# Two tiles through the first products together: x loaded ahead of the weights, k, v and q as double products

## The chip, the core and the metric

The kernel runs on one core of a Trainium2 chip. The metric is the device time of one execution in microseconds; a time of a kernel is the median of its runs. All times inside an execution are microseconds from the start of the profiled span. The core's engines are TensorE (PE, with its weight loads as PEld), VectorE (DVE), ScalarE (ACT), GpSimd (POOL) and SyncE (SP), which issues all the DMA of this kernel.

## The reference

Two layers, run twice with the same weights: a linear attention block and a PEER expert block, each with a layernorm in front and a residual behind. Tokens 2048, width 576, 32 heads of 18.

```python
x = A_x
x = x + _A_ref(_layernorm(x, axis=-1), A_wqkv, A_wo)
x = x + _B_ref(_layernorm(x, axis=-1), B_w_q, B_k1, B_k2, B_u, B_v)
x = x + _A_ref(_layernorm(x, axis=-1), A_wqkv, A_wo)
x = x + _B_ref(_layernorm(x, axis=-1), B_w_q, B_k1, B_k2, B_u, B_v)
```

In `_A_ref`, q, k and v are the three 576-column thirds of `layernorm(x) @ wqkv`. With phi(t) = (t + 1 for t > 0, else exp(t)) + 1e-6, each head sums phi(k)^T v over all tokens (the state), multiplies it by phi(q) and divides by phi(q) times the sum of phi(k); the result goes through wo. Only the very first products of the first layer, for tokens 0 to 383, are touched by the change.

## The kernel before

**Tiles.** The 2048 tokens are 16 tiles of 128. A tile of x is one load of 288 KB; it is normalized, transposed by TensorE in five blocks of 128 columns (576 columns, with 64 of the third block doubled), and multiplied by the weights.

**Two parts of every number.** Each transposed tile and each weight block is split into a high part, rounded by ScalarE (`split`, L110, or L115 for the third block), and a low part, the difference, by VectorE (L111, or L116; one block of k by GpSimd). A product (`product`, L220) adds up 14 passes of two matmuls each: five of high by high, four of high by low weight, five of low tile by high weight. With `by_block` the passes are sorted by weight block, so that a product can start when block 0 of the weights is there; before, only k of tile 0 uses it. In the profile `thif` and `tlof` are the parts of a tile, `whi` and `wlo` those of the weights, `ptf` the transposition, `ppk`, `ppv`, `ppq` the products.

**Weights.** `load_weight` (L134 to L137) loads five blocks for each of k, v and q, in six transfers, since the third block is loaded in two halves. They go to ten staging buffers: k and v fill them, and q's blocks reuse those of k, after k's splits. Later the `fold` loads reuse v's.

**Order.** On TensorE, ScalarE, VectorE and GpSimd the instructions run in the order in which the program writes them (`in_order`). SP's order is set by a planner at build time, from its own estimate of what is ready when. In the profile SP issues x of tile 0, the identity, k's blocks (six transfers), x of tile 1, v's blocks (six), x of tile 2, q's blocks (six), `kraw` (a small table of expert keys), two further small tables, x of tile 3, and then the first `fold` loads; counted in this order, x of tile 1 is the ninth transfer, `kraw` the twenty-third.

**The start.** 14 warm-up matmuls run on TensorE while the first load is under way. Then the program writes: statistics of tile 0 (`statistics`, L166 to L174: three small operations on VectorE, two on GpSimd, one on VectorE), normalization (`normalized`, L195, on ScalarE), transposition, two warm-up matmuls, k of tile 0 (block by block), tile 1's transposition, k of tile 1, v of tile 0 and 1, the state of tile 0 (`front_state`, L291), tile 2's transposition, q of tile 0, the state of tile 1, q of tile 1. Between them stand the weights' splits. k and q go through `phi` (L226 to L228: exp on ScalarE, two operations on VectorE); v is copied from PSUM by ScalarE in three pieces (L251, L253). `small_loads` gives GpSimd a row of preparations: two memsets, then L609, then L611, which waits for `kraw`, and three memsets and two copies behind it (the last is L621). Tile 2's statistics come behind these on GpSimd.

PSUM is four buffers of two banks each, shared by transpositions, products, warm-ups and the state sums; the state keeps one for as long as the first layer's loop lasts. From tile 2 on a loop takes one tile after the other (k, v, q, transposition of the next, state), together with the loads and products of the `fold`.

Of the kernel before, what the change touches and what calls it, by code (L numbers as in the profile page):

```python
# [27 lines left out]
CUT = 2 * HC  # L28
# [11 lines left out]
def blocks(rem):  # L40

    rows, at = [], 0
    for b in range(NB):
        rows.append((at, b - (b > rem)))
        at += 64 if b == rem else P
    return rows


def passes(rem):
    rest = [b for b in range(NB) if b != rem]  # L50
    return ([("hi", b, "hi") for b in range(NB)] + [("hi", b, "lo") for b in rest]
            + [("lo", b, "hi") for b in range(NB)])
# [6 lines left out]
def network(ctx, tc, x_in, wqkv, wo, wq_t, k_t, u_t, v2, c_mask, c_mask4, c_ident, c_code, c_code1, c_scale, c_shift, out):  # L59
# [7 lines left out]
    def psum(name):  # L67
        return ps.tile([P, 1024], F32, tag="ps", name=name)
# [5 lines left out]
        return t[:, 512 - CUT:512 - CUT + D]  # L74

    PARTS = (0, CUT, 512 - CUT), (CUT, D, 512)


    ident = cp.tile([P, P], F32, name="ident")
# [47 lines left out]
    def load_weight(src, c0, rem, name):  # L127

        tiles = []
        for b, (r, bl) in enumerate(blocks(rem)):  # L130
            st = stage(f"{name}st{c0}_{b}")
            cols = slice(c0, c0 + D)
            if b != rem:
                nc.sync.dma_start(st, src[r:r + P, cols])  # L134
            else:
                nc.sync.dma_start(st[:64], src[r:r + 64, cols])
                nc.sync.dma_start(st[64:], src[r:r + 64, cols])  # L137
            tiles.append(st)
        return tiles

    def split_weight(tiles, c0, hi, lo, rem, which=range(NB), eng=nc.vector):
        for b in which:
            cols = slice(c0, c0 + D)
            if b != rem:
                split(tiles[b], hi[:, b, cols], lo[:, blocks(rem)[b][1], cols], eng)
            else:
                split_mixed(tiles[b], hi[:, b, cols])
# [13 lines left out]
                                  reason="in_order")  # L161


    def statistics(xt, n, soon=False):
        st = wk.tile([P, 2, 6], F32, tag="st", name=f"st{n}")
        nc.vector.bn_stats(st[:, 0], xt[:, :HALF])  # L166
        nc.vector.bn_stats(st[:, 1], xt[:, HALF:])
        mv = wk.tile([P, 2], F32, tag="mv", name=f"mv{n}")
        nc.vector.bn_aggr(mv, st.rearrange("p a b -> p (a b)"))  # L169
        rs = wk.tile([P, 2], F32, tag="rs", name=f"rs{n}")  # L170
        nc.gpsimd.tensor_scalar(rs[:, 0:1], mv[:, 1:2], EPS_LN, 1.0, op0=ALU.add, op1=ALU.mult)  # L171
        nc.gpsimd.tensor_tensor(rs[:, 0:1], rs[:, 0:1], mhalf, op=ALU.pow)
        eng = nc.vector if soon else nc.gpsimd
        eng.tensor_scalar(rs[:, 1:2], mv[:, 0:1], rs[:, 0:1], -1.0, op0=ALU.mult, op1=ALU.mult)  # L174
        return rs

    def spread(xt, total, n):

# [9 lines left out]
        nc.gpsimd.tensor_tensor(rs[:, 1:2], m[:, 0:1], rs[:, 0:1], op=ALU.mult)  # L188
        return normalized(xt, rs, n)

    def normalized(xt, rs, n):

        y = wk.tile([P, 2, 320], F32, tag="y", name=f"y{n}", bufs=3)
        x2 = bass.AP(tensor=xt.tensor, offset=xt.offset, ap=[xt.ap[0], [256, 2], [1, 320]])
        nc.scalar.activation(y, x2, AF.Identity, scale=rs[:, 0:1], bias=rs[:, 1:2])  # L195
        return y.rearrange("p a b -> p (a b)")

    def transposed(y, n, more=None, tag="t", step=P):
# [11 lines left out]
        split(pt[:, :w], hi.rearrange("p a b -> p (a b)")[:, :w], lo.rearrange("p a b -> p (a b)")[:, :w])  # L210
        return hi, lo

    def product(tt, hi, lo, cols, n, parts=PARTS, rem=REM, by_block=False):

        o = psum(f"pp{n}")
        todo = sorted(passes(rem), key=lambda p: p[1]) if by_block else passes(rem)
        for i, (a, b, w) in enumerate(todo):
            wb = hi[:, b] if w == "hi" else lo[:, blocks(rem)[b][1]]
            for c0, c1, at in parts:
                nc.tensor.matmul(o[:, at:at + c1 - c0], tt[a == "lo"][:, b, :], wb[:, cols + c0:cols + c1],  # L220
                                 start=(i == 0), stop=(i == len(todo) - 1))
        return o

    def phi(p, n):
# [8 lines left out]
    ys = {}  # L233
    kva = {}
    wob = {}


    def front_T(l, t):
        tt["f", l, t] = yield from transposed(ys.pop(("f", l, t)), f"f{l}_{t}")

    def front_k(l, t):
        k = product(tt["f", l, t], whi, wlo, D, f"k{l}_{t}", by_block=(l == 0 and t == 0))
        yield
        tt["fk", l, t] = phi(k, f"k{l}_{t}")

    def front_v(l, t):
        v = product(tt["f", l, t], whi, wlo, 2 * D, f"v{l}_{t}", parts=((0, CUT, 0), (CUT, D, 512)))
        yield
        vt = v5[t % 2]
        for c, x in ((0, v[:, :2 * HC]), (4, v[:, 512:512 + 2 * HC])):  # L250
            nc.scalar.activation(vt[:, c:c + 4, :63], x.rearrange("p (c e) -> p c e", c=4), AF.Copy)  # L251
        yield
        nc.scalar.activation(vt[:, 8:, :36], v[:, 512 + 2 * HC:512 + 2 * HC + 72].rearrange("p (c e) -> p c e", c=2), AF.Copy)  # L253

    def front_q(l, t):
        q = product(tt["f", l, t], whi, wlo, 0, f"q{l}_{t}")
        yield
        fq = phi(q, f"q{l}_{t}")
        nc.sync.dma_start(pq_d[l][t], fq)
# [331 lines left out]
    def warm_up(n):  # L591

        p = psum("warm")
        for i in range(n):
            nc.tensor.matmul(p[:, :512], junk[:, :P], junk[:, :512], start=True, stop=True)

    def first_load(l, t):
        xt = wk.tile([P, D], F32, tag="x", name=f"xf_{t}", bufs=3)
        nc.sync.dma_start(xt, x_in[t * P:(t + 1) * P, :])
        xs["f", t] = xt  # L600

    def first_ln(l, t):
        xt = xs.pop(("f", t))
        ys["f", 0, t] = normalized(xt, statistics(xt, f"f0_{t}"), f"f0_{t}")

    def small_loads():
        for t in v5:
# [47 lines left out]
    def run(l, *seq):  # L655


        for f, t, *n in seq:
            if f is bc or ok(t):
                g = begun.pop((f, l, t), None) or (exp_T(l, *t) if f is bc else f(l, t))  # L660
                for i in range(n[0] if n else 99):
                    if g is None or next(g, bc) is bc:
                        break
                else:
                    begun[f, l, t] = g
# [31 lines left out]
    first_load(0, 0)  # L697
    nc.vector.memset(junk, 0.0)
    nc.sync.dma_start(ident, c_ident)
    wk_in = load_weight(wqkv, D, REM, "w")  # L700
    first_load(0, 1)
    wv_in = load_weight(wqkv, 2 * D, REM, "w")
    ET = mybir.EngineType
    ALL = ET.PE, ET.Activation, ET.DVE, ET.Pool
    with in_order(*ALL):
        x0, x1 = xs.pop(("f", 0)), xs.pop(("f", 1))
        warm_up(14)
        rs0 = statistics(x0, "f0_0", soon=True)
        split_weight(wk_in, D, whi, wlo, REM, (0,))
        ys["f", 0, 0] = normalized(x0, rs0, "f0_0")  # L710
        split_weight(wk_in, D, whi, wlo, REM, (1, 2))
        run(0, (fT, 0, 1))
        warm_up(2)
        run(0, (fT, 0))
        split_weight(wk_in, D, whi, wlo, REM, (3,), nc.gpsimd)
        rs1 = statistics(x1, "f0_1", soon=True)
        split_weight(wk_in, D, whi, wlo, REM, (4,))
        ys["f", 0, 1] = normalized(x1, rs1, "f0_1")
        run(0, (k, 0, 1), (fT, 1))
        split_weight(wv_in, 2 * D, whi, wlo, REM, (0, 1))  # L720
        run(0, (k, 0), (k, 1, 1))
        split_weight(wv_in, 2 * D, whi, wlo, REM, (2, 3, 4))
        first_load(0, 2)
        wq_in = load_weight(wqkv, 0, REM, "w")
        small_loads()
        first_load(0, 3)
        run(0, (k, 1), (v, 0, 1))
        split_weight(wq_in, 0, whi, wlo, REM, (0, 1))
        run(0, (v, 0))
        first_ln(0, 2)  # L730
        split_weight(wq_in, 0, whi, wlo, REM, (2, 3))
        run(0, (v, 1, 1))
        split_weight(wq_in, 0, whi, wlo, REM, (4,))
        run(0, (st, 0), (fT, 2), (v, 1), (q, 0), (st, 1), (q, 1))
        PER, FIRST = 8, 13
        for t in range(2, FIRST):
            m0 = PER * (t - 2)
            groups = [m for m in range(m0, m0 + PER) if m < 2 * H]
            done = (m0 - 1) // 16 if m0 % 16 == 0 and 0 < m0 <= 2 * H else None
            for m in groups:  # L740
                fold_load(m)
            if t + 2 < NT:
                first_load(0, t + 2)
            if t + 1 < NT:
                first_ln(0, t + 1)
            run(0, (k, t, 1))
            if done is not None:
                fold_out(done)
            run(0, (k, t))
            run(0, (v, t, 1))  # L750
            if done is not None and groups:
                fold_T(done)
            run(0, (v, t))
            if groups:
                run(0, (q, t), (fT, t + 1), (st, t))
            elif t < L:
                run(0, (fT, t + 1), (q if t < L - 1 else st, t), (st if t < L - 1 else q, t if t < L - 1 else -1))
            if done is not None and not groups:
                fold_T(done)
            for m in groups:  # L760
                fold_mm(m)
# [101 lines left out]
```

## Time and profile before

| what | value |
|---|---|
| runs | 745.76, 747.09, 747.62 us; median 747.09 |
| the profiled execution | 748.71 us, span 746.9 us |
| mean granted TensorE clock | 0.995 |
| busy: PE, PEld, DVE, ACT, POOL | 726.5, 675.2, 458.9, 289.7, 200.4 us |

The profile comes from one execution of its own. Busy times overlap between engines and don't add up to the span. A row of a timeline gives the start, the duration, the engine, the line, the operation, what is written and read, and in brackets the idle time of the engine before it and what ended that. A row with x2 or more is several instructions merged, with the duration from the first start to the last end. The chain of waits is read from the last instruction back, and shown in order of time: the work that set the end.

### The profile page before, as it was taken

How to read it: one execution, taken by the hardware profiler on the slowest of the kernel's cores; microseconds unless marked ns; L12 is line 12 of the kernel's file. 1: busy time of each engine (PE TensorE's matmuls, PEld its weight loads, DVE VectorE, ACT ScalarE, POOL GpSimd, SP SyncE). 2: the span in 40 equal slices, each digit the busy share in tenths (PEclk: the TensorE clock that was granted, in tenths of full speed). 3: DMA queues.
4: the chain of work that ended last, by engine and by line, in shares of the span. 5: the costliest groups of instructions: out<-in, count | busy, mean ns of one | idle time of the engine just before them, and what ended most of it. 6: DMA issues, size and time to landing. Idle time of an engine off the chain costs nothing.

```text
span 746.9 us, 14647 instructions
## 1 busy us (share of the span) xinstructions
PE 726.5 (97%) x5672; PEld 675.2 (90%) x5672; DVE 458.9 (61%) x1006; ACT 289.7 (39%) x588; POOL 200.4 (27%) x541
## 2 busy tenths in 40 slices
PE   7999999999999999999999999999999999999995
PEld 4999999999998889999999999999899999999884
DVE  3732332324236887666666666563366899999986
ACT  4523232332324544444444444452233333444343
POOL 2110001000003543333333333130033334533431
PEclk9999999999999999999999999999999999999998
DMA  9727546641121321222333212222634323121101
GB/s 256 251 81 247 197 159 216 232 130 50 49 64 32 111 99 68 99 86 83 89 104 105 87 68 84 84 72 68 176 87 119 104 83 116 32 88 41 48 33 65
DMA packets 52470, 79.64 MB, mean 107 GB/s; under 512 B 5616, under 2 KB 22512, under 8 KB 52400
## 3 DMA queue, kind: packets, MB, share of 16 engines
q1 hardware_dynamic: 52400, 78.70, 33.1%
q8 instruction: 45, 0.74, 0.4%
q14 instruction: 25, 0.20, 0.1%
HBM read 55.12 MB, written 23.56 MB: 105 GB/s over the span
## 4 chain that ended last, share of the span: by engine, by line
PE 82%; DVE 10%; ACT 3%; issue 2%; POOL 1%; DMA 1%; SPq 0%; DVEq 0%; POOLq 0%; ACTq 0%
PE ppk L220 15%; PE ppv L220 15%; PE ppq L220 13%; PE ppo L414 13%; PE pps L444 12%; PE kva L291 3%; PE fold_ps L560 2%; PE ptb L205 2%; PE ptf L205 2%; PE pto L205 2%; PE po L528 2%; DMA wst<-in_wqkv 1%; PE m L345 1%; DVE o L392 1%; DVE tlob L111 1%
## 5 line engine op out<-in xcount | busy, mean ns | idle before, releaser
L227 DVE TENSOR_SCALAR ek<-ek 128x576 f32<-128x576 f32 x32 | 15.1, 472 | 82.5 <-ACT ek L226 82.5
L220 PE MATMUL ppk<-whi,thif 128*128 128x252 f32 x320 | 50.3, 302 | 2.4 <-ACT thif L110 2.3
L220 PEld LDWEIGHTS ppk<-whi,thif 128*128 128x128 f32 x320 | 44.6, 191 | 6.8 <-ACT thif L110 3.4
L414 PE MATMUL ppo<-ohi,thio 126*128 126x252 f32 (+1 forms) x320 | 50.2, 299 | 0.1
L171 POOL TENSOR_SCALAR rsf<-mvf 128x1 f32<-128x1 f32 x16 | 3.1, 192 | 171.2 <-DVE mvf L169 171.0
L220 PE MATMUL ppk<-whi,tlof 128*128 128x252 f32 x320 | 48.2, 295 | 0.3 <-DVE tlof L111 0.3
L227 DVE TENSOR_SCALAR eq<-eq 128x576 f32<-128x576 f32 x32 | 15.6, 488 | 52.5 <-ACT eq L226 52.5
L220 PE MATMUL ppv<-whi,thif 128*128 128x252 f32 x320 | 47.4, 294 | 0.1
L220 PE MATMUL ppv<-whi,tlof 128*128 128x252 f32 x320 | 46.9, 293 | 0.0
L195 ACT ACTIVATE yb<-x,rsb 128x640 f32<-128x640 f32 x32 | 29.5, 923 | 44.3 <-POOL rsb L188 44.2
L444 PE MATMUL pps<-shi,thib 128*128 128x512 f32 x160 | 43.9, 404 | 2.0 <-ACT thib L110 2.0
L414 PEld LDWEIGHTS ppo<-ohi,thio 126*128 126x128 f32 (+1 forms) x320 | 44.8, 189 | 1.1 <-DVE eq L228 0.3
L220 PEld LDWEIGHTS ppk<-whi,tlof 128*128 128x128 f32 x320 | 44.9, 190 | 0.5 <-DVE tlof L111 0.5
L220 PEld LDWEIGHTS ppv<-whi,thif 128*128 128x128 f32 x320 | 43.9, 188 | 0.4 <-ACT thif L110 0.3
L220 PEld LDWEIGHTS ppv<-whi,tlof 128*128 128x128 f32 x320 | 43.9, 188 | 0.0
L181 ACT ACTIVATE junk<-x,mb 128x576 bf16<-128x576 f32 x32 | 24.7, 771 | 49.5 <-POOL mb L180 46.1
L444 PE MATMUL pps<-shi,tlob 128*128 128x512 f32 x160 | 42.7, 397 | 0.0
L449 ACT ACTIVATE s<-pps 128x512 f32<-128x512 f32 x32 | 19.1, 596 | 54.9 <-PE pps L444 54.9
L251 ACT ACTIVATE v<-ppv 128x252 f32<-128x252 f32 x64 | 20.9, 379 | 50.0 <-PE ppv L220 50.0
L220 PE MATMUL ppq<-whi 128*128 128x252 f32 (+1 forms) x260 | 39.6, 299 | 0.6 <-DVE eq L228 0.6
L404 DVE SCALAR_TENSOR_TENSOR x<-po,x 128x576 f32<-128x576 f32 x29 | 21.9, 753 | 29.3 <-PE po L528 28.3
L414 PE MATMUL ppo<-olo,thio 126*128 126x252 f32 (+1 forms) x256 | 39.5, 293 | 0.0
(155 smaller groups left out, 1788.9 us busy)
## 6 DMA issues: line engine op xcount, KB each, us to landing
fold<-in_wq_t SPq DMA_DIRECT2D x64, 288.0 KB, 4.8
whi<-hl_d SPq DMA_DIRECT2D x26, 320.0 KB, 3.4
pq_d<-eq SPq DMA_DIRECT2D x19, 288.0 KB, 2.2
pq<-pq_d SPq DMA_DIRECT2D x19, 288.0 KB, 3.1
xf<-in_x SPq DMA_DIRECT2D x16, 288.0 KB, 5.4
x<-in_x SPq DMA_DIRECT2D x16, 288.0 KB, 2.7
x_d<-x SPq DMA_DIRECT2D x16, 288.0 KB, 3.3
x<-x_d SPq DMA_DIRECT2D x16, 288.0 KB, 2.7
```

The costliest lines, as they stand in the source:

```text
L181: nc.scalar.activation(junk, xt, AF.Square, bias=m[:, 0:1], accum_out=m[:, 1:2])
L195: nc.scalar.activation(y, x2, AF.Identity, scale=rs[:, 0:1], bias=rs[:, 1:2])
L205: nc.tensor.transpose(pt[:, b * P:(b + 1) * P], x, ident)
L220: nc.tensor.matmul(o[:, at:at + c1 - c0], tt[a == "lo"][:, b, :], wb[:, cols + c0:cols + c1], start=(i == 0), stop=(i == len(todo) - 1))
L227: nc.vector.tensor_scalar(e, e, 1.0, EPS, op0=ALU.min, op1=ALU.add)
L251: nc.scalar.activation(vt[:, c:c + 4, :63], x.rearrange("p (c e) -> p c e", c=4), AF.Copy)
L291: nc.tensor.matmul(a[64 * h:64 * h + 64, c * 72:c * 72 + n], vt[:, 2 * c + h], fk[:, f0:f0 + n], start=(t == 0 and c == 0), stop=(t == NT ...
L404: nc.vector.scalar_tensor_tensor(y, row(p), 0.0, xt, op0=ALU.add, op1=ALU.add, accum_out=total)
L414: nc.tensor.matmul(p[:, at:at + c1 - c0], hl[a][:r, b], w[:r, c0:c1], start=(i == 0), stop=(i == len(todo) - 1))
L444: nc.tensor.matmul(p[:, :512], hl[a == "lo"][:, b, :], shi[:, b] if w == "hi" else slo[:, blocks(REM)[b][1]], start=(i == 0), stop=(i == l ...
L449: nc.scalar.activation(s[:, NE:], p[:, :512], AF.Copy)
L528: nc.tensor.matmul(p[:, at:at + c1 - c0], c[i], vmix[:, c0:c1], start=(i == 0 and not based), stop=(i == 1))
```

## The change

x of tile 1 is loaded third, ahead of all weights. The statistics of both tiles stand at the head of the program; the third small operation on GpSimd replaces the one on VectorE. Tile 0 is normalized by ScalarE, tile 1 by VectorE. Both tiles are transposed before the first product. `pair_product` computes the same product for both tiles at once, into two PSUM buffers: the passes sorted by weight block, each for tile 0 and then for tile 1. k, v and q of tiles 0 and 1 are made this way, with the splits of the weight blocks and the evictions of the products placed between them; both states follow behind q. Tile 2 is normalized and transposed between v and q.

```diff
...
-        eng = nc.vector if soon else nc.gpsimd
-        eng.tensor_scalar(rs[:, 1:2], mv[:, 0:1], rs[:, 0:1], -1.0, op0=ALU.mult, op1=ALU.mult)
-        return rs
+        nc.gpsimd.tensor_scalar(rs[:, 1:2], mv[:, 0:1], rs[:, 0:1], -1.0, op0=ALU.mult, op1=ALU.mult)
+        yield rs
...
+        if vector:
+            nc.vector.tensor_scalar(y, x2, rs[:, 0:1], rs[:, 1:2], op0=ALU.mult, op1=ALU.add)
+        else:
+            nc.scalar.activation(y, x2, AF.Identity, scale=rs[:, 0:1], bias=rs[:, 1:2])
...
+    def pair_product(t0, t1, cols, n, parts=PARTS):
+
+        o = [psum(f"pp{n}0_{t}") for t in (0, 1)]
+        todo = sorted(passes(REM), key=lambda p: p[1])
+        for i, (a, b, w) in enumerate(todo):
+            wb = whi[:, b] if w == "hi" else wlo[:, blocks(REM)[b][1]]
+            for p, tt in zip(o, (t0, t1)):
+                for c0, c1, at in parts:
+                    nc.tensor.matmul(p[:, at:at + c1 - c0], tt[a == "lo"][:, b, :], wb[:, cols + c0:cols + c1],
+                                     start=(i == 0), stop=(i == len(todo) - 1))
+        return o
...
     nc.sync.dma_start(ident, c_ident)
+    first_load(0, 1)
     wk_in = load_weight(wqkv, D, REM, "w")
-    first_load(0, 1)
     wv_in = load_weight(wqkv, 2 * D, REM, "w")
...
         warm_up(14)
-        rs0 = statistics(x0, "f0_0", soon=True)
+        st0, st1 = statistics(x0, "f0_0"), statistics(x1, "f0_1")
+        next(st0)
+        rs0 = next(st0)
+        next(st1)
+        rs1 = next(st1)
+        ys["f", 0, 0] = normalized(x0, rs0, "f0_0")
+        ys["f", 0, 1] = normalized(x1, rs1, "f0_1", vector=True)
         split_weight(wk_in, D, whi, wlo, REM, (0,))
-        ys["f", 0, 0] = normalized(x0, rs0, "f0_0")
-        split_weight(wk_in, D, whi, wlo, REM, (1, 2))
         run(0, (fT, 0, 1))
         warm_up(2)
-        run(0, (fT, 0))
+        run(0, (fT, 0), (fT, 1, 1))
+        split_weight(wk_in, D, whi, wlo, REM, (1,))
+        run(0, (fT, 1))
+        warm_up(2)
+        split_weight(wk_in, D, whi, wlo, REM, (2,))
         split_weight(wk_in, D, whi, wlo, REM, (3,), nc.gpsimd)
-        rs1 = statistics(x1, "f0_1", soon=True)
         split_weight(wk_in, D, whi, wlo, REM, (4,))
-        ys["f", 0, 1] = normalized(x1, rs1, "f0_1")
-        run(0, (k, 0, 1), (fT, 1))
+        front_pair("k", D)
         split_weight(wv_in, 2 * D, whi, wlo, REM, (0, 1))
-        run(0, (k, 0), (k, 1, 1))
-        split_weight(wv_in, 2 * D, whi, wlo, REM, (2, 3, 4))
         first_load(0, 2)
         wq_in = load_weight(wqkv, 0, REM, "w")
         small_loads()
         first_load(0, 3)
-        run(0, (k, 1), (v, 0, 1))
-        split_weight(wq_in, 0, whi, wlo, REM, (0, 1))
-        run(0, (v, 0))
-        first_ln(0, 2)
-        split_weight(wq_in, 0, whi, wlo, REM, (2, 3))
-        run(0, (v, 1, 1))
-        split_weight(wq_in, 0, whi, wlo, REM, (4,))
-        run(0, (st, 0), (fT, 2), (v, 1), (q, 0), (st, 1), (q, 1))
+        split_weight(wv_in, 2 * D, whi, wlo, REM, (2,))
+        run(0, (k, 0))
+        split_weight(wv_in, 2 * D, whi, wlo, REM, (3,))
+        run(0, (k, 1))
+        x2 = xs.pop(("f", 2))
+        st2 = statistics(x2, "f0_2")
+        next(st2)
+        split_weight(wv_in, 2 * D, whi, wlo, REM, (4,))
+        front_pair("v", 2 * D, PARTS_V)
+        ys["f", 0, 2] = normalized(x2, next(st2), "f0_2")
+        split_weight(wq_in, 0, whi, wlo, REM, (0,))
+        run(0, (fT, 2, 1), (v, 0))
+        split_weight(wq_in, 0, whi, wlo, REM, (1,))
+        run(0, (v, 1))
+        split_weight(wq_in, 0, whi, wlo, REM, (2, 3, 4))
+        run(0, (fT, 2))
+        front_pair("q", 0)
+        run(0, (st, 0), (st, 1), (q, 0), (q, 1))
...
```

More of the change, by code (lines that the diff above doesn't have):

```diff
@@ L76, in network @@
     PARTS = (0, CUT, 512 - CUT), (CUT, D, 512)
+    PARTS_V = (0, CUT, 0), (CUT, D, 512)
     ident = cp.tile([P, P], F32, name="ident")
@@ L161, in in_order, with statistics @@
                                   reason="in_order")
-    def statistics(xt, n, soon=False):
+    def statistics(xt, n):
         st = wk.tile([P, 2, 6], F32, tag="st", name=f"st{n}")
@@ L169, in statistics @@
         nc.vector.bn_aggr(mv, st.rearrange("p a b -> p (a b)"))
+        yield
         rs = wk.tile([P, 2], F32, tag="rs", name=f"rs{n}")
@@ L189, in layernorm_sum, with normalized @@
         return normalized(xt, rs, n)
-    def normalized(xt, rs, n):
+    def normalized(xt, rs, n, vector=False):
         y = wk.tile([P, 2, 320], F32, tag="y", name=f"y{n}", bufs=3)
         x2 = bass.AP(tensor=xt.tensor, offset=xt.offset, ap=[xt.ap[0], [256, 2], [1, 320]])
-        nc.scalar.activation(y, x2, AF.Identity, scale=rs[:, 0:1], bias=rs[:, 1:2])
+        if vector:
+            nc.vector.tensor_scalar(y, x2, rs[:, 0:1], rs[:, 1:2], op0=ALU.mult, op1=ALU.add)
+        else:
+            nc.scalar.activation(y, x2, AF.Identity, scale=rs[:, 0:1], bias=rs[:, 1:2])
         return y.rearrange("p a b -> p (a b)")
@@ L211, in transposed, with product @@
         return hi, lo
-    def product(tt, hi, lo, cols, n, parts=PARTS, rem=REM, by_block=False):
+    def product(tt, hi, lo, cols, n, parts=PARTS, rem=REM):
         o = psum(f"pp{n}")
-        todo = sorted(passes(rem), key=lambda p: p[1]) if by_block else passes(rem)
+        todo = passes(rem)
         for i, (a, b, w) in enumerate(todo):
@@ L235, in network @@
     wob = {}
+    pairs = {}
     def front_T(l, t):
@@ L241, in front_k, with front_pair @@
     def front_k(l, t):
-        k = product(tt["f", l, t], whi, wlo, D, f"k{l}_{t}", by_block=(l == 0 and t == 0))
+        k = pairs.pop(("k", l, t), None)
+        if k is None:
+            k = product(tt["f", l, t], whi, wlo, D, f"k{l}_{t}")
         yield
         tt["fk", l, t] = phi(k, f"k{l}_{t}")
+    def front_pair(f, cols, parts=PARTS):
+        pairs[f, 0, 0], pairs[f, 0, 1] = pair_product(tt["f", 0, 0], tt["f", 0, 1], cols, f, parts)
     def front_v(l, t):
-        v = product(tt["f", l, t], whi, wlo, 2 * D, f"v{l}_{t}", parts=((0, CUT, 0), (CUT, D, 512)))
+        v = pairs.pop(("v", l, t), None)
+        if v is None:
+            v = product(tt["f", l, t], whi, wlo, 2 * D, f"v{l}_{t}", parts=PARTS_V)
         yield
@@ L255, in front_q @@
     def front_q(l, t):
-        q = product(tt["f", l, t], whi, wlo, 0, f"q{l}_{t}")
+        q = pairs.pop(("q", l, t), None)
+        if q is None:
+            q = product(tt["f", l, t], whi, wlo, 0, f"q{l}_{t}")
         yield
@@ L603, in first_ln @@
         xt = xs.pop(("f", t))
-        ys["f", 0, t] = normalized(xt, statistics(xt, f"f0_{t}"), f"f0_{t}")
+        *_, rs = statistics(xt, f"f0_{t}")
+        ys["f", 0, t] = normalized(xt, rs, f"f0_{t}")
     def small_loads():
```

## The prediction

> **What bounds the kernel now.** I read the page first, then the chain of waits for the first 60 us, since the diff touches nothing later, then the timelines of SP, ACT, DVE, POOL and PE for that stretch, and last the table by windows for TensorE's clock.
>
> ```profile
> span 746.9 us, 14647 instructions
> ...
> PE 82%; DVE 10%; ACT 3%; issue 2%; POOL 1%; DMA 1%; SPq 0%; DVEq 0%; POOLq 0%; ACTq 0%
> ```
> ```profile
> 3.19 6.45 DMA wst<-in_wqkv
> ...
> 12.11 4.99 PE ppk L220 x24
> 17.10 0.56 PE ptf L205 x5
> ...
> 18.44 3.92 PE ppk L220 x28
> 22.36 7.28 PE ppv L220 x56
> 29.65 0.74 PE kva L291 x20
> ...
> 39.62 3.64 PE ppk L220 x28
> ```
>
> The whole is TensorE's: 82% of the chain. Up to 18.44 us the chain is made of loads, a slow product (k of tile 0, 24 matmuls in 4.99 us) and a transposition; from 18.44 on PE runs almost without a hole, and at 39.62 it begins k of tile 2, the first instruction that both kernels share. So the question is only when PE gets there. The work before it is the same in both: six products of 28 matmuls, at 7.28/56 = 0.130 us each 3.64 us a product, 21.8 in all, plus two states (0.74 each) and three transpositions (0.56 each). A lead that is won by then is kept: the rest of the program is unchanged, and its chain is mostly PE's.
>
> ```profile
> 8.33 0.77 PE L205 MATMUL ptf<-ident,yf 128*128 128x128 f32 x5 [1.72 <-ACT yf L195]
> 8.94 0.59 PE L595 MATMUL warm<-junk 128*128 128x512 bf16 x2
> 11.05 0.54 PE L220 MATMUL ppk<-whi,thif 128*128 128x252 f32 x2 [1.52 <-ACT thif L110]
> ```
> ```profile
> 5.70:9.10 3.40, 1.68 (x10) 0.89 (x9) 0.84 (x2) 2.18 (x3) 0.00 (x0) 1.00 1.02 249
> 9.10:12.50 3.40, 1.62 (x9) 0.96 (x8) 2.79 (x5) 2.42 (x4) 0.85 (x1) 1.00 1.07 342
> 12.50:15.90 3.40, 3.40 (x16) 3.40 (x16) 1.37 (x4) 0.92 (x1) 2.59 (x6) 0.51 1.05 290
> ```
>
> The windows' columns are: stretch, its length, then busy time with count for PE, PEld, DVE, ACT and POOL, the granted clock, the DMA share and GB/s. After a stretch in which PE was busy for 1.62 of 3.40 us, the clock was 0.51 for one such stretch, though 1.68 of 3.40 just before had not cost it. Part of the 4.99 us of k is this half clock.
>
> **Loads.** What SP issues, and when:
>
> ```profile
> 8.38 0.47 SPq L136 DMA_DIRECT2D wst<-in_wqkv  x1
> ...
> 11.83 1.60 SPq L134 DMA_DIRECT2D wst<-in_wqkv  x2
> ...
> 16.87 0.36 SPq L610 DMA_DIRECT2D kraw<-in_k_t  x1
> ...
> 21.14 0.80 SPq L550 DMA_DIRECT2D fold<-in_wq_t  x2
> ```
> ```profile
> 6.79 0.68 ACT L110 ACTIVATE whi<-wst 128x576 fp32r<-128x576 f32 x1 [4.77 <-DMA wst<-in_wqkv]
> ...
> 8.39 0.68 ACT L110 ACTIVATE whi<-wst 128x576 fp32r<-128x576 f32 x1
> ...
> 19.43 0.64 ACT L226 ACTIVATE ek<-ppk 128x576 f32<-128x576 f32 x1
> ...
> 26.10 0.65 ACT L251 ACTIVATE v<-ppv 128x252 f32<-128x252 f32 x2 [1.90 <-PE ppv L220]
> 26.64 0.24 ACT L253 ACTIVATE v<-ppv 128x72 f32<-128x72 f32 x1
> 29.29 0.92 ACT L195 ACTIVATE yf<-xf,rsf 128x640 f32<-128x640 f32 x1 [2.41 <-POOL rsf L174]
> 30.12 0.67 ACT L115 ACTIVATE whi<-wst 128x576 fp32r<-128x576 f32 x1
> 30.69 1.24 ACT L110 ACTIVATE whi<-wst 128x576 fp32r<-128x576 f32 x2
> ```
>
> Eight transfers are in flight at a time here: the twelfth goes out at 8.38, when the fourth (block 1 of k) has landed, and ACT takes that block at 8.39. So landings follow from the place in the queue and the bytes ahead. The third place landed at about 6.7 (block 0), the fourth at 8.36, the bytes through block 2 at 9.64 (3.19 + 6.45), the ninth (x of tile 1) by 11.8, which releases the seventeenth. With x of tile 1 third, it lands at 6.7 instead of 11.8, block 0 of k at 8.36 instead of 6.7, block 1 at 9.64, block 4 by 11.8. From the ninth place on nothing moves: v, x of tile 2, q and kraw land as before.
>
> **k.** DVE's and POOL's rows:
>
> ```profile
> 3.55 0.46 DVE L166 BATCH_NORM_STATS2 stf<-xf 128x6 f32<-128x288 f32 x1 [2.39 <-DMA xf<-in_x]
> ...
> 4.41 0.21 DVE L169 BATCH_NORM_AGGREGATE mvf<-stf 128x2 f32<-128x12 f32 x1
> ...
> 11.23 0.82 DVE L111 TENSOR_TENSOR tlof<-ptf,thif 128x640 fp32r<-128x640 f32 x1
> ...
> 19.16 1.42 DVE L111 TENSOR_TENSOR wlo<-wst,whi 128x576 fp32r<-128x576 f32 x2
> 20.50 0.45 DVE L227 TENSOR_SCALAR ek<-ek 128x576 f32<-128x576 f32 x1
> 20.98 0.76 DVE L228 SCALAR_TENSOR_TENSOR ek<-ppk,ek 128x576 f32<-128x576 f32 x1
> ...
> 27.74 0.21 DVE L169 BATCH_NORM_AGGREGATE mvf<-stf 128x2 f32<-128x12 f32 x1
> ```
> ```profile
> 23.05 0.33 POOL L611 TENSOR_TENSOR kpad<-kraw 128x14 f32<-128x14 f32 x1 [7.79 <-DMA kraw<-in_k_t]
> ...
> 24.86 0.53 POOL L621 COPY pick<-ident 128x128 f32<-128x128 f32 x2
> 28.04 0.19 POOL L171 TENSOR_SCALAR rsf<-mvf 128x1 f32<-128x1 f32 x1 [2.65 <-DVE mvf L169]
> ```
>
> Tile 0 normalizes before block 0's split and is transposed near 7 us; its last statistics operation goes from DVE to POOL, which is within the 1.34 below. Tile 1's statistics take 1.07 us (3.55 to 4.62) from 6.7, and 1.34 pass from the end of an aggregate to the start of a normalization (27.95 to 29.29, POOL's three small operations): 9.1. Its normalization on VectorE isn't in this trace; the nearest row is the 128x576 TENSOR_SCALAR, 0.45, so 0.50 for 640 columns; 0.92, ACT's time for the same, is the upper end, and it can't be under the 0.45. At 9.6 DVE is free, and behind y of tile 1 are queued, in the written order, lo of block 0 (0.71), lo of tile 0 (0.82), lo of block 1 (0.71), lo of tile 1 (0.82): 12.7, with gaps 12.8. ACT, with two splits and two evictions of tiles from 8.4 on, each like the 0.68 of its row at 8.39, is done by 11.2. PE does the two transpositions and the second pair of warm-up matmuls (0.59) in this wait; without the wait the warm-up would cost its 0.6. Block 0's last pass for tile 1 needs lo of tile 1, so at 12.8 two of its matmuls and blocks 1 to 4 are left, 46 x 0.130 = 6.0: both k end at 18.8, not 22.36. Blocks 3 and 4 are split by about 14, ahead of PE.
>
> **v.** 56 matmuls back to back: 18.8 + 7.3 = 26.1. The block 4 split is queued on DVE behind both phi(k) and the statistics of tile 2: 18.8 + exp 0.64 + (0.45 + 0.76) x 2 + 0.71 (block 3) + statistics 1.07 + 0.71 = 24.4, with gaps up to 24.7. PE reads that lo at about 25.0. It just holds; a miss costs its own length. The statistics end at 23.7 to 23.8.
>
> **The new wait: T2.** After v PE transposes tile 2, and its normalization needs POOL. POOL, in written order, first does the small preparations, and these stand behind kraw, which lands at 23.05 as before; they end at 25.39 (24.86 + 0.53). Then 28.04 to 29.29 is 1.25 from POOL's first operation to ACT's normalization: y of tile 2 starts at 26.65, though by the statistics alone it would be 23.8 + 1.34 = 25.15. PE waits from 26.1 to 27.6.
>
> **q.** ACT has, behind y of tile 2: block 0 of q, three copies of v of tile 0, block 1, three of tile 1, block 2. By starts, y costs 0.83 (29.29 to 30.12), a split 0.6 (30.12 to 30.69), the copies 0.78 (26.10 to 26.88). PE transposes 27.6 to 28.15, takes block 0 at 28.2, and for tile 1 needs a free PSUM buffer: the four hold both v, the transposition and q of tile 0, so it waits for v of tile 0 to be copied, until 28.9. From there blocks 0 and 1 take 22 x 0.130 to 31.75; block 2 has been split at 26.65 + 0.83 + 2 x 0.6 + 2 x 0.78 + 0.68 + 0.76 = 31.7 (the last two for its split and its subtraction, taken as 0.76 like the other DVE rows of two operands). Then 32 x 0.130 = 4.2 and two states, 1.5: 37.4. Against 39.62 that is **2.2 us**. In this execution: span 744.7 for 746.9. The execution itself took 748.71, 1.6 over the median of the runs shown, 747.09; off the median, **744.9**.
>
> What makes this sturdy: POOL's 25.39 hangs on a landing, not on k. k may end 1.4 later, by a late x, a dear y or a half clock, before the statistics, not POOL, set the end.
>
> **Rivals.** (a) *POOL is free.* SP's order is not written out, a planner sets it; if kraw goes ahead of q's blocks, or of some, T2 hangs on the statistics: 25.15, all of q 1.5 earlier, end 35.9, gain 3.7: 743.4. For it: the splits that free q's staging buffers come later now, so the planner may find kraw ready first. Against: before, it kept the written order.
> (b) *The clock falls in q.* From 26.1 to 28.9 PE waits 2.0 of 2.8 us, so a stretch of 3.4 that covers this has about 1.4 busy, less than the 1.62 that cost a half-clock stretch. That takes 1.7: gain 0.5, 746.6. The stretch must lie over the whole wait, 3.4 against 2.8: with a free phase, about one run in five. The same size comes if the median run of before had no half clock in k: 24 matmuls at 0.130 are 3.1 us, not 4.99, so the change has up to 1.9 less to win.
> [...]
> (c) *kraw goes out later.* POOL's queue then holds tile 2's normalization, ACT's queue everything behind it, PE T2 and q. From a landing at 25.25 (2.2 after 23.05) the change loses. If x of tile 3 and two fold loads go ahead (issue 21.94 rather than 16.87), it lands 5.1 later: end 42.5, 2.9 slower, 750.0. For it: before, the mask loads were moved behind just those.
> (d) *The change doesn't do what it says:* the planner keeps x of tile 1 ninth. Landing at 11.8, DVE's queue ends at 17.9, k at 23.9, statistics 28.9, T2 follows, end about 41.0: 1.4 slower, 748.5.
>
> **How the numbers follow.** Forecast 0.42, (a) 0.22, (b) 0.19, (c) 0.12, (d) 0.05. About 0.3%, 2.2 us, is what a measurement of this kernel can tell from no change; the runs before span 1.9. The forecast lies on that edge, so half of it counts as faster: 0.21 + 0.22 = 0.43. (c) goes past it, 0.11. The rest, 0.46, is within. The likeliest case's own range is 743.9 to 746.0, by 0.4 for y, 0.6 for v's block 4 and half a us for landings. The asked range runs from just under (a), 743.2, to 748.0, over (b) and the upper runs of before; it leaves out (c) and most of (d).
>
> **What would show it.** x of tile 1 read by DVE near 6.7 and block 0 by ACT near 8.4; the first k pair stopped on lo of tile 1 near 12.8; both k done near 19, v near 26; POOL's kpad on kraw near 23, and T2 released by it after 27; k of tile 2 at 37.4. If POOL's kpad runs before 20, (a); a window under 0.9 after 26, (b); kpad after 25, (c). If PE waits within v for block 4, the sum of v is wrong. If k of tile 2 begins near 37.4 and the time has not moved, then a lead isn't kept, and the first premise is wrong.

## The result, and the profile after

| kernel | median, us | lowest to highest | runs | ratio to before, 95% interval |
|---|---|---|---|---|
| before | 746.83 | 745.76 to 749.07 | 17 | |
| changed | 747.89 | 745.94 to 751.18 | 17 | 1.0017 [1.0009, 1.0025] |

The change costs 1.1 us by the medians and 0.17% by the ratio: under the 0.3% that I had set as a bound, but the interval of the ratio excludes a gain. The forecast was a gain of 2.2. The changed kernel's profiled execution, 747.89 us with a span of 746.0, is its median; the one of before, 748.71 with 746.9, lies 1.9 above before's median. So the two spans, compared alone, show a gain of 0.9 that the medians don't.

The page after, its span and its chain by engine, and then the chain of waits up to k of tile 2:

```profile
span 746.0 us, 14651 instructions
...
PE 76%; DVE 12%; ACT 4%; POOL 3%; DMA 3%; issue 2%; SPq 0%; DVEq 0%; POOLq 0%; ACTq 0%
```
```profile
16.66 5.98 DMA kraw<-in_k_t
...
22.78 0.37 POOL kpad L638
...
24.36 0.47 POOL pick L648 x2
...
24.92 0.20 POOL rsf L173
...
26.16 0.93 ACT yf L199
27.09 0.04 issue
27.13 1.22 PE ptf L209 x5
28.36 8.43 PE ppq L236 x56
36.79 1.36 PE kva L317 x40
38.15 3.85 PE ppk L224 x28
```

The first 28 us of the chain no longer contain a product. They are loads, the last of them that of kraw, then GpSimd's preparations behind it, GpSimd's part of tile 2's statistics, its normalization, its transposition. The double product of q then takes 8.43 us, where 56 matmuls at 0.130 are 7.3. The timelines of DVE and PE, for the part ahead of that wait:

```profile
5.52 0.46 DVE L167 BATCH_NORM_STATS2 stf<-xf 128x6 f32<-128x288 f32 x1 [0.76 <-DMA xf<-in_x]
...
7.90 0.61 DVE L197 TENSOR_SCALAR yf<-xf,rsf 128x640 f32<-128x640 f32 x1 [1.32 <-POOL rsf L175]
...
10.66 0.82 DVE L112 TENSOR_TENSOR tlof<-ptf,thif 128x640 fp32r<-128x640 f32 x1
```
```profile
17.63 0.68 PE L236 MATMUL ppv<-whi,thif 128*128 128x252 f32 x4
...
24.39 0.69 PE L236 MATMUL ppv<-whi,tlof 128*128 128x252 f32 x4
27.13 1.22 PE L209 MATMUL ptf<-ident,yf 128*128 128x128 f32 x5 [2.06 <-ACT yf L199]
...
38.08 1.58 PE L224 MATMUL ppk<-whi,thif 128*128 128x252 f32 x10
```

Both k are done at 17.6 and both v at 25.1, each about a microsecond earlier than forecast. Then PE stands still for 2.06 us. The windows show what this does (columns as in the prediction):

```profile
23.87:27.29 3.42, 1.36 (x11) 1.13 (x10) 0.00 (x0) 1.13 (x2) 1.99 (x7) 1.00 0.26 53
27.29:30.70 3.41, 3.41 (x16) 3.41 (x16) 2.07 (x3) 3.41 (x11) 0.00 (x0) 0.50 0.88 295
30.70:34.11 3.41, 3.41 (x28) 3.41 (x27) 2.37 (x4) 1.16 (x2) 0.00 (x0) 1.00 1.01 376
```

PE is busy for 1.36 of 3.42 us, and through the next 3.41 the clock is 0.50: 16 matmuls, where 28 run in the 3.41 us at 1.00 behind it.

### The profile page after: what moved, and what is told of

Same layout as the page of the kernel before. It is cut to its first block, busy times and chain, and to the rows that moved or that the text cites. A ratio compares the mean times of both kernels' runs of the same rounds, so it can differ in the third digit from the quotient of the medians.

```text
span 746.0 us, 14651 instructions
## 1 busy us (share of the span) xinstructions
PE 726.9 (97%) x5674; PEld 675.4 (91%) x5674; DVE 460.1 (62%) x1005; ACT 288.9 (39%) x587; POOL 200.7 (27%) x543
## 4 chain that ended last, share of the span: by engine, by line
PE 76%; DVE 12%; ACT 4%; POOL 3%; DMA 3%; issue 2%; SPq 0%; DVEq 0%; POOLq 0%; ACTq 0%
PE ppk L224 14%; PE ppv L224 14%; PE ppo L440 12%; PE ppq L224 11%; PE pps L470 10%; PE kva L317 3%; PE fold_ps L586 2%; PE ptf L209 2%; PE ptb L209 2%; PE pto L209 2%; DMA wst<-in_wqkv 2%; PE po L554 2%; PE ppq L236 1%; DVE x L430 1%; DVE o L418 1%
## 5 line engine op out<-in xcount | busy, mean ns | idle before, releaser
L224 PE MATMUL ppk<-whi,thif 128*128 128x252 f32 (+1 forms) x300 | 45.9, 299 | 0.1
L224 PE MATMUL ppv<-whi,thif 128*128 128x252 f32 (+1 forms) x300 | 44.4, 295 | 0.1
L224 PEld LDWEIGHTS ppk<-whi,thif 128*128 128x128 f32 x300 | 41.0, 188 | 3.8 <-issue 3.3
L224 PE MATMUL ppv<-whi,tlof 128*128 128x252 f32 (+1 forms) x300 | 43.9, 293 | 0.0
L224 PE MATMUL ppk<-whi,tlof 128*128 128x252 f32 (+1 forms) x300 | 43.9, 293 | 0.0
L224 PEld LDWEIGHTS ppv<-whi,thif 128*128 128x128 f32 x300 | 41.2, 188 | 0.4 <-ACT thif L111 0.3
L224 PEld LDWEIGHTS ppk<-whi,tlof 128*128 128x128 f32 x300 | 41.2, 188 | 0.0
L224 PEld LDWEIGHTS ppv<-whi,tlof 128*128 128x128 f32 x300 | 41.2, 188 | 0.0
```

## The experiments

Two theories stood against each other. C: the lead in the two first traces is an accident of the one execution of before (a half-clock stretch inside k of tile 0), while the changed kernel pays for the wait at tile 2 and mostly for a half clock behind it. L: the changed start is earlier in every execution, and the lead is lost after 40 us. "k of tile 2" below is the start of its first matmul in PE's timeline: 39.45 in the first trace of before, 38.08 in the first of the changed kernel. (In the chain of waits the same start reads 39.62 and 38.15; below, all starts are from the timeline.)

The runs come in series, each with runs of before beside it. Before's own median was 746.83 us in the result above, 746.52 for the two repeats, e1 and e2, 746.37 for e3 to e6, and 745.99, on another chip, for e7 and e8. So across series the ratios to before compare better than the medians.

**Both kernels again.**

> The kernel before, unchanged, for the spread of its runs and a second trace. Theory C (clock): the lead of the change exists in the one trace of before only because that execution had a half-clock stretch inside k of tile 0; in most executions the stretch falls where TensorE waits anyway or does not fall at all. Then this trace starts k of tile 2 at 37.7 to 38.6 instead of 39.62, and runs with a mean granted clock near 0.998 are 1 to 2 us shorter than those near 0.995. Theory L (later): before always starts k of tile 2 near 39.6, and the change loses its lead after 40 us.

> The changed kernel, unchanged. Theory C: k of tile 2 starts near 38.1 when the clock falls behind the wait for tile 2's transposition and near 36.5 when it does not; the median is 0.5 to 1.5 us over before, and the runs' spans go with their granted clocks. Theory L: k of tile 2 starts near 38.1 or earlier in every execution and the rest of the program is 1 to 2 us longer than in before.

Before: 746.64 us (12 runs; the 34 other runs of before in this series had 746.52). PE's timeline, first of the first trace, then of this one:

```profile
12.11 0.54 PE L220 MATMUL ppk<-whi,tlof 128*128 128x252 f32 x2 [0.26 <-DVE tlof L111]
...
16.94 0.71 PE L205 MATMUL ptf<-ident,yf 128*128 128x128 f32 x5
...
39.45 1.46 PE L220 MATMUL ppk<-whi,thif 128*128 128x252 f32 x10
```

```profile
11.11 0.53 PE L220 MATMUL ppk<-whi,tlof 128*128 128x252 f32 x2 [0.26 <-DVE tlof L111]
11.47 0.42 PE L220 MATMUL ppk<-whi,thif 128*128 128x252 f32 x2
...
14.65 0.71 PE L205 MATMUL ptf<-ident,yf 128*128 128x128 f32 x5
...
36.89 1.32 PE L220 MATMUL ppk<-whi,thif 128*128 128x252 f32 x9
```

k of tile 2 begins at 36.89, not 39.45. Of the 2.56 us, 1.00 comes from loads that landed earlier (this row of k at 11.11 instead of 12.11; ScalarE took block 2 of k at 8.73 instead of 9.72) and 1.29 from the clock: from here to the transposition k takes 3.54 us instead of 4.83, since no half-clock stretch fell (1.00 in every window from 4.37 to 14.61). The last 0.27 is a wait in q of tile 0 that is shorter in this trace. The span is 744.4, against 746.9.

The changed kernel: 748.25 us (12 runs), 1.0016 [1.0007, 1.0026]; k of tile 2 at 38.86, its half-clock stretch again behind the wait (2.06 us of idle up to 27.46, then 0.50 from 29.13 to 32.55). The runs sorted by their mean granted clock, before's 46 of this series and the changed kernel's 29 of this series and the result: before with 0.998 or more, 19 runs, median 746.3; with 0.997, 14 runs, 746.5; with 0.996 or less, 13 runs, 747.7. Changed with 0.998 or more, 8 runs, 747.1; with 0.997, 10 runs, 748.5; with 0.996 or less, 11 runs, 748.5. (A half clock near the kernel's end counts in this mean too, as the 0.50 from 743.0 to the end in before's first trace, so it sorts only roughly.) Even among its best executions the changed kernel is no faster. Theory C fits; the earlier start of L isn't there.

**GpSimd freed for tile 2 (e1).**

```diff
         nc.sync.dma_start(kraw, k_t)
+        nc.sync.dma_start(code_w, c_code)
+        nc.sync.dma_start(shift, c_shift)
+        yield
         nc.gpsimd.tensor_tensor(kpad[:, :, 25:32], kraw[:, :, 1:], ...
...
-        nc.sync.dma_start(code_w, c_code)
-        nc.sync.dma_start(shift, c_shift)
+        yield
...
-        small_loads()
+        small = small_loads()
+        next(small)
...
         ys["f", 0, 2] = normalized(x2, next(st2), "f0_2")
+        next(small)
```

> The changed kernel with GpSimd's preparations (everything that stands behind the load of kraw) moved behind the small operations of tile 2's normalization. Theory C: the wait for tile 2's transposition (2.06 us) and the half-clock stretch behind it (1.7 us) both go; k of tile 2 starts at 34.4 to 35.2, and the median falls 3 us under the changed kernel and 1.5 to 2.5 us under before. Theory L: k of tile 2 starts there too, but the time stays within 1 us of the changed kernel, since a lead is lost later on.

745.12 us (10 runs, 744.75 to 745.54), 0.998 [0.9971, 0.9989]: 3.1 under the changed kernel, 1.4 under before. GpSimd's and PE's timelines:

```profile
22.87 0.52 POOL L173 TENSOR_SCALAR rsf<-mvf 128x1 f32<-128x1 f32 x1 [8.67 <-DVE mvf L170]
...
24.36 0.21 POOL L641 TENSOR_TENSOR kpad<-kraw 128x14 f32<-128x14 f32 x1
```
```profile
24.65 0.69 PE L236 MATMUL ppv<-whi,tlof 128*128 128x252 f32 x4
25.41 0.77 PE L209 MATMUL ptf<-ident,yf 128*128 128x128 f32 x5
...
35.25 0.92 PE L224 MATMUL ppk<-whi,thif 128*128 128x252 f32 x5
```

The statistics no longer wait for kraw, the transposition follows v almost at once, the clock holds (0.999 in the mean of this execution; four matmuls of q go by in 0.52 us from 28.08, against 0.97 from 29.12 at the changed kernel's half clock), and k of tile 2 begins at 35.25. A queue order of three small operations turns the change from a loss into a gain. The lead arrives at the end: its span of 743.1 is 1.3 under that of before's second trace, for a start 1.64 earlier. So L falls, except for 0.36 that is lost on the way to q of tile 11 (e6 and e7). The runs spread over 0.8 us, those of the changed kernel in the same series over 3.1.

**Warm-ups in the wait, twice (e2, e3).**

```diff
         ys["f", 0, 2] = normalized(x2, next(st2), "f0_2")
+        warm_up(9)
```

> The changed kernel with 9 warm-up matmuls on TensorE (about 0.2 us each) in the wait between v and tile 2's transposition; nothing else differs. Theory C: the wait stays (transposition near 27.1), the half-clock stretch behind it goes; k of tile 2 starts at 36.2 to 36.8, the median falls by 1 to 1.7 us to about before's. Theory L: k of tile 2 moves likewise, the time does not.

748.36 us, 1.003 [1.0018, 1.0042]: not what C said. PE's timeline and the windows:

```profile
25.08 2.12 PE L621 MATMUL warm<-junk 128*128 128x512 bf16 x8
27.47 0.77 PE L209 MATMUL ptf<-ident,yf 128*128 128x128 f32 x5 [0.28 <-ACT yf L199]
28.70 0.53 PE L236 MATMUL ppq<-whi,thif 128*128 128x252 f32 x2 [0.46 <-ACT v L277]
29.94 0.75 PE L236 MATMUL ppq<-whi,thif 128*128 128x252 f32 x2 [0.70 <-ACT v L277]
```
```profile
26.67:30.08 3.41, 1.97 (x11) 1.00 (x10) 1.51 (x2) 3.41 (x10) 0.00 (x0) 1.00 0.82 254
30.08:33.50 3.42, 3.42 (x15) 3.42 (x16) 2.92 (x4) 2.12 (x4) 0.00 (x0) 0.50 0.98 332
```

The warm-ups fill the wait, but they take a PSUM buffer of their own, and now both halves of q wait for copies of v: tile 0's until 28.70, tile 1's until 29.94. The half clock comes all the same (0.50 from 30.08 to 33.50), and k of tile 2 begins only at 40.10. This execution took 750.22 us, 1.9 over e2's median, so it need not be typical; that the buffer causes the two waits is read from e3, which has neither. This edit changed two things; e3 puts the same matmuls into the transposition's own buffer:

```diff
         pt = psum(f"pt{n}")
+        for i in range(warm):
+            nc.tensor.matmul(pt[:, :512], junk[:, :P], junk[:, :512], start=True, stop=True)
...
-        tt["f", l, t] = yield from transposed(ys.pop(("f", l, t)), f"f{l}_{t}")
+        tt["f", l, t] = yield from transposed(ys.pop(("f", l, t)), f"f{l}_{t}", warm=9 if (l, t) == (0, 2) else 0)
```

> The changed kernel with 9 warm-up matmuls in the wait ahead of tile 2's transposition, as before, but into the transposition's own PSUM buffer, so that the buffers of q stay where they were. Theory C splits the loss: the half clock in q is what lifts the changed kernel from about 747.1 (its executions with a clock of 0.999) to 748.3. Then k of tile 2 starts at 36.6 to 37.5, and the median falls by about 1 us to 747.0 to 747.4, still not under before's 746.5, since the wait of 2.06 us stays. If the clock has no part in it, the median stays at 748.2 and the start at 38.1 or later.

```profile
25.08 2.12 PE L209 MATMUL ptf<-junk 128*128 128x512 bf16 x8
27.30 0.76 PE L211 MATMUL ptf<-ident,yf 128*128 128x128 f32 x5
27.87 1.20 PE L238 MATMUL ppq<-whi,thif 128*128 128x252 f32 x4
...
37.12 1.07 PE L226 MATMUL ppk<-whi,thif 128*128 128x252 f32 x6
```

747.07 us (11 runs), 1.0007 [0.9998, 1.0016]. The wait is as long as in the changed kernel, the clock holds (1.00 from 25.39 to 32.21), and k of tile 2 begins at 37.12, 1.0 and 1.7 before the changed kernel's two traces. This separates the two costs, roughly: the half clock is worth 0.8 to 1.2 us by the medians (747.89 or 748.25 without the warm-ups), but 0.7 by the ratios (1.0017 and 1.0016 against 1.0007), whose intervals overlap. The wait and its effects are the 1.95 to e1, or 1.87 between the two starts of k of tile 2.

**Before without its accident (e4).**

```diff
         run(0, (fT, 0, 1))
-        warm_up(2)
+        warm_up(7)
```

> The kernel before with 7 warm-up matmuls in place of 2 behind tile 0's transposition, in TensorE's wait ahead of k. Theory C: no half clock in k in any execution; k of tile 2 starts at 37.0 to 37.3, the median falls by 0.2 to 0.5 us to that of before's executions with a clock of 0.998 and over (746.3), and the upper group of its runs near 747.8 disappears. If the half clock in k does not set that upper group, it stays.

746.11 us (11 runs, 745.62 to 746.73) against 746.37 (26 runs, to 748.16): the upper group is gone, k of tile 2 begins at 36.81. The median moves within its interval, 0.9996 [0.9988, 1.0005], as it should if most executions of before never had the half clock in k.

**The loads' order undone (e5), on top of e1.**

```diff
-    first_load(0, 1)
     wk_in = load_weight(wqkv, D, REM, "w")
+    first_load(0, 1)
```

> The version with GpSimd freed (e1), with x of tile 1 loaded ninth again, behind all of k's weights. If the order of the loads carries the gain: x of tile 1 lands near 11.8, the k pair can begin its part for tile 1 only near 17, both k end near 23, k of tile 2 starts near 40, and the time is 4 to 5 us over e1, 749 to 750. If the double products carry it by themselves, the time stays within 1 us of e1's 745.1.

751.14 us (5 runs), 1.0061 [1.0048, 1.0074], 6 over e1. DVE's timeline and PE's:

```profile
10.98 0.46 DVE L167 BATCH_NORM_STATS2 stf<-xf 128x6 f32<-128x288 f32 x1 [6.16 <-DMA xf<-in_x]
```
```profile
14.03 1.33 PE L209 MATMUL ptf<-ident,yf 128*128 128x128 f32 x5 [5.72 <-DVE yf L197]
...
41.94 1.59 PE L224 MATMUL ppk<-whi,thif 128*128 128x252 f32 x10
```

x of tile 1 is there 5.5 us later than in the changed kernel (10.98 for 5.52), everything in VectorE's written order waits behind its normalization, and PE runs slowly on top, as at a half clock (the transposition at 14.03 takes 1.33 us, where the changed kernel's at 8.57 takes 0.77; four matmuls of k take 0.96 from 16.98 and 0.52 from 18.87 on), which makes the loss larger than I expected. The double products need the early load; by themselves they lose.

**Tile 2's transposition behind q (e6), on top of e1.**

```diff
-        ys["f", 0, 2] = normalized(x2, next(st2), "f0_2")
-        next(small)
-        split_weight(wq_in, 0, whi, wlo, REM, (0,))
-        run(0, (fT, 2, 1), (v, 0))
-        split_weight(wq_in, 0, whi, wlo, REM, (1,))
+        split_weight(wq_in, 0, whi, wlo, REM, (0, 1))
+        run(0, (v, 0))
+        split_weight(wq_in, 0, whi, wlo, REM, (2,))
         run(0, (v, 1))
-        split_weight(wq_in, 0, whi, wlo, REM, (2, 3, 4))
-        run(0, (fT, 2))
+        split_weight(wq_in, 0, whi, wlo, REM, (3, 4))
+        ys["f", 0, 2] = normalized(x2, next(st2), "f0_2")
+        next(small)
         front_pair("q", 0)
-        run(0, (st, 0), (st, 1), (q, 0), (q, 1))
+        run(0, (fT, 2), (st, 0), (st, 1), (q, 0), (q, 1))
```

> e1 with tile 2's normalization and transposition moved behind the products of q, and with three blocks of q split ahead of the eviction of v. TensorE then has no wait between v (end near 25.1) and q: k of tile 2 at 34.4 to 34.8 against e1's 35.25, the median 0.4 to 0.8 us under e1, 744.3 to 744.7. If q's blocks or a PSUM buffer hold TensorE instead, k of tile 2 stays at 35.2 or later and so does the time.

744.87 us (11 runs), 0.9977 [0.9968, 0.9986]. k of tile 2 begins at 34.50 as expected, 0.75 before e1, but only 0.25 of it is in the median. The list of PE's waits says where half of it went: "ppq <- DVE ek" is 0.7 us in e1 and 1.1 here, and q of tile 11 begins only 0.36 before e1's (174.73 for 175.09).

**A lead given back at tile 11 (e7, e8), on top of e6.** That wait stands in every kernel at one place: q of tile 11 needs a PSUM buffer, k of tile 11 still holds one, and its exp stands in ScalarE's queue behind the normalization of tile 12. The wait is 0.50 to 0.52 in before, e4 and e5, and 0.73 to 0.75 in the changed kernel, e1, e2 and e3. (My expectations number these tiles 12 and 13; they are 11 and 12.)

```diff
-        nc.gpsimd.tensor_scalar(rs[:, 1:2], mv[:, 0:1], rs[:, 0:1], -1.0, op0=ALU.mult, op1=ALU.mult)
+        eng = nc.vector if soon else nc.gpsimd
+        eng.tensor_scalar(rs[:, 1:2], mv[:, 0:1], rs[:, 0:1], -1.0, op0=ALU.mult, op1=ALU.mult)
...
-        st0, st1 = statistics(x0, "f0_0"), statistics(x1, "f0_1")
+        st0, st1 = statistics(x0, "f0_0", True), statistics(x1, "f0_1", True)
```

> e6 with the third small statistics operation of tiles 0 and 1 on VectorE again, as before, so that GpSimd runs two instructions fewer. In every trace with it on GpSimd, except that of e5, the step from aggregate to GpSimd's last operation for tile 13 takes 1.42 to 1.44 us instead of 1.18 to 1.20, and q of tile 12 waits 0.7 to 1.1 instead of 0.5. If the two instructions are the reason, the step falls back to 1.2, the wait by 0.2 to 0.4, and the median to 744.4 to 744.7. If not, all three stay at e6's values, 1.43, 1.1 and 744.9.

744.18 us (8 runs), 0.9973 [0.9963, 0.9984], the fastest version here: 1.8 under before. Against e6 its median is 0.7 lower, but on another chip, where before was 0.4 lower too; by the ratios to before it is 0.3, inside both intervals. The traces say 0.41 at q of tile 11, although k of tile 2 begins 0.33 later (34.83 for 34.50). The rows of GpSimd, VectorE and PE ahead of q of tile 11, of e6 and then of e7:

```profile
170.28 0.19 POOL L173 TENSOR_SCALAR rsf<-mvf 128x1 f32<-128x1 f32 x1 [15.92 <-DVE mvf L170]
...
173.91 0.76 DVE L244 SCALAR_TENSOR_TENSOR ek<-ppk,ek 128x576 f32<-128x576 f32 x1 [0.46 <-PE ptf L209]
...
174.73 1.59 PE L224 MATMUL ppq<-whi,thif 128*128 128x252 f32 x10 [1.12 <-DVE ek L244]
```
```profile
170.23 0.19 POOL L173 TENSOR_SCALAR rsf<-mvf 128x1 f32<-128x1 f32 x1 [15.55 <-DVE mvf L170]
...
173.50 0.76 DVE L245 SCALAR_TENSOR_TENSOR ek<-ppk,ek 128x576 f32<-128x576 f32 x1
...
174.32 1.57 PE L225 MATMUL ppq<-whi,thif 128*128 128x252 f32 x10 [0.39 <-DVE ek L245]
```

GpSimd's step for tile 12, from the end of the aggregate to its last operation, fell from 1.43 to 1.08, and the wait from 1.12 to 0.39. That is two things, of about 0.36 each. GpSimd begins the step 0.36 sooner after the aggregate. And VectorE no longer stops between its two operations in k's `phi`, for 0.46 us in e6 and 0.10 in e7; e1 has 0.11 there, so this is also what e6's wait has over e1's. (The profile puts the stop down to tile 12's transposition, but in e7 the operation starts ahead of that transposition's end, at 173.93.) Moving two small instructions at the head from GpSimd to VectorE, 160 us earlier, took both away in this trace. That their number sets it is not shown: the step is 1.18 to 1.20 in before and e4, where GpSimd runs as few of them as in e7, and 1.18 in e5, where it runs as many as in e6. The cause is open.

```diff
-            if t + 1 < NT:
+            if t + 1 < NT and t != 12:
                 first_ln(0, t + 1)
...
             run(0, (k, t))
+            if t == 12:
+                first_ln(0, t + 1)
```

> e6 with the normalization of tile 13 written behind the eviction of k of tile 12 instead of ahead of it, so that ScalarE takes exp(k) as soon as k is done. If q of tile 12 waits because its PSUM buffer is k's and exp(k) stands in ScalarE's queue behind the normalization, the wait falls from 1.1 to under 0.3 and the median by 0.6 to 1.0, to 743.9 to 744.3. If another thing holds it, the wait and the time stay.

747.39 us (11 runs), 1.0016 [1.0007, 1.0026]: slower than before, where e6 was faster (0.9977). By my wrong count this moved the next tile's normalization: the wait at 175 stays at 1.12, and a new one of 1.96 us appears at the transposition of tile 13, which now finds no normalized tile.

## Why the prediction was wrong

**The step that failed** is the subtraction "Against 39.62 that is 2.2 us" and, after it, "off the median, 744.9". 39.62 is the start of k of tile 2 in one execution, whose total I had noted as 1.6 over the median. I took the difference from the disturbed trace and laid it on the median of others. Before's second trace has 36.89 for 39.45: 1.29 of it is the half clock that I had myself read in the windows, 1.00 earlier loads, 0.27 a shorter wait in q. Against 36.89 the same forecast, 37.4, is a loss of 0.3 to 0.5 us, not a gain of 2.2. That most executions of before are like the second trace, its runs and e4 show: 26 runs of before have a median of 746.37 and reach 748.16, and with the wait filled the highest of 11 is 746.73.

**The new time was nearly right.** I gave 37.4 for k of tile 2. With the clock held (e3) it is 37.12; with the half clock, 38.08 and 38.86. Term by term: x of tile 1 was there at 5.5, not 6.7; its normalization on VectorE took 0.61, between my 0.50 and 0.92; lo of tile 1 ended at 11.5, not 12.8; k ended at 17.6, not 18.8, v at 25.1, not 26.1, without a hole at block 4; GpSimd took kraw at 22.78, not 23.05; the transposition began at 27.13, not 27.6. That k came a microsecond early gained nothing, as the prediction said it would not: the end hung on kraw. PE's wait, 1.5 us in the sum (26.1 to 27.6), became 2.06, since v was early.

**Rival (b) was the other half.** I gave the half clock in q 0.19, "about one run in five", and 0.5 of gain left. It came in both traces of the changed kernel (0.50 from 27.29 and from 29.13), and e3 prices it at 0.7 to 1.2 us. That a stretch must lie over the whole wait, with a free phase, was my assumption, and no run shows it; what the two traces show is a wait of 2.06 us, longer than in the sum, and the half clock behind it. And (b)'s last sentence, that the median run of before might have no half clock in k, was the truth and got no chance of its own; it was no rival but the baseline.

**What decides a drop** is not the busy share of the 3.4 us ahead of it alone, as rival (b) took it. In before's second trace PE was busy for 1.58 of 3.41 us and the clock stayed at 1.00 behind that, to 14.61; in before's first trace 0.51 stood behind 1.62 of 3.40 us, in e2 0.50 behind 1.97 of 3.41. The first two windows of before's second trace:

```profile
4.37:7.78 3.41, 1.58 (x8) 0.49 (x5) 1.17 (x4) 1.40 (x2) 0.74 (x2) 1.00 1.00 260
7.78:11.20 3.42, 2.09 (x12) 1.36 (x12) 2.55 (x5) 3.09 (x6) 0.54 (x1) 1.00 1.01 361
```

Nor is it the length of one wait alone: that trace has an idle of 1.98 us on PE ahead of 7.93 and kept its clock, before's first trace lost it with none longer than 1.72 in the two windows ahead, the changed kernel behind one of 2.06 in both traces. What else counts stays open. Before's half clock lasts from 12.5 to 15.9, the changed kernel's from 27.29 to 30.70 in its first trace and from 29.13 to 32.55 in its second, about 3.4 us each; e2's begins at 30.08. So it came at another time in each execution.

**Rivals (a), (c) and (d).** The planner kept kraw where it was (16.66) and put x of tile 1 third, so none of these happened by themselves. e1 builds (a) by GpSimd's order instead of SP's: k of tile 2 at 35.25, where I had 35.9. e5 builds (d) on top of e1, so without the wait for kraw: 41.94, where I had about 41.0. (c) wasn't tried.

**The first premise held, with a dent.** A lead is kept to the end, but 0.36 us of it is lost between k of tile 2 and q of tile 11 in the changed kernel, e1 and e3 alike: 0.12 inside k of tile 2, and 0.24 by the longer wait at tile 11, which the prediction didn't look for. Together, against before's second trace: 0.23 at k of tile 2 (37.12 to 36.89) and these 0.36 make 0.6, and e3's median is 0.7 over before; the half clock adds the rest.

## What to carry to other kernels

Before a change is subtracted from a trace, look whether that execution is a typical one: here its own time, 1.9 us over the median, was as large as everything that the change could win. Ask of each wait that a change leaves on TensorE not only how long it is, but whether the clock falls afterwards (to 0.50 here, behind 2.06 us in both traces). A faster stage is worth nothing when the next one hangs on a landing; the gain came only when three small operations were moved ahead of the queue's head that waited for it.

## What the runs showed of the hardware

Filling a wait of PE with junk matmuls kept the clock up (1.00 from 25.39 to 32.21) and cost no time of its own (e3: the transposition behind them at 27.30, against 27.13 and 27.46 without them), but a PSUM buffer for them did (e2: two waits of 0.46 and 0.70 us). GpSimd's step from the end of the aggregate to the start of its last small operation takes 1.08 us at the tiles on both sides of tile 12 in the first traces of before and of the changed kernel. At tile 12 it takes 1.41 to 1.44 in the changed kernel, e1, e2, e3, e6 and e8, 1.18 to 1.20 in before, e4 and e5, and 1.08 in e7; why is open.
